# Linear-attention block with a gated MLP: joined feature stores and loads, and another order of the pair loop

## The chip, the cores and the metric

The kernel runs on one core of a Trainium2 chip. The metric is the time of one execution in device microseconds. Before the change it is 2499.09 us (median of 3 runs, 2498.96 to 2500.07).

## The reference

```python
xn = _layernorm(x)                                    # x: 2048 tokens x 1024
q, k, v = split(xn @ wqkv)                            # 32 heads of 32
pq, pk = q @ w_phi, k @ w_phi                         # per head, 32 x 32
phi_q = concat(softmax(pq), softmax(-pq))             # 64 features a head
phi_k = concat(softmax(pk), softmax(-pk))
kv, z = phi_k.T @ v, sum over tokens of phi_k         # per head
o = (phi_q @ kv) / (phi_q @ z + 1e-6)
s = o @ wo
g = silu(((sigmoid(xn @ w_gate)) * (xn @ w_up)) @ w_down)   # 3584 hidden
return x + s * g
```

All in float32. Every large product is made of three matmuls: each operand is split in a high part (rounded to the matmul's float32 form) and the low rest, and hi x hi, hi x lo and lo x hi are added up (`mm3`, L148).

## The kernel before, in words

Large matrix products go through a seven-product scheme (Strassen's in Winograd's form) on blocks of 2 x 2. The seven products are named B11, T2, T3, B21, T1, T4, B22. B11, T2, T3 and T1 open a bank of PSUM; B21 adds on to B11's bank, T4 to T3's, B22 to T1's. In the product with `wo` these four banks are banks 4 to 7, in the order in which the products open them.

The stages, in order: layer norm and the K and V projections; the Q projection; gate and up projections with the gated product in several passes; then the two stages that the change touches.

**The down stage** (from L1820 on) is the product with `w_down`: 112 steps (`dsteps`), each with one block of weights and one or two blocks of hidden values, loaded from DRAM (`down_load`, L941) and split by ScalarE and VectorE (`down_prep`, L959). The first 84 steps have two halves of 12 matmuls each, the last 28 one half. Between halves the kernel calls `tick()` (L178), a clock of the program: `later(n, f)` (L160) puts work n ticks ahead, and all of a tick's work comes, in program order, after what the engines were given before it. So this order, and not the time at which data are there, sets the order of SP's DMA queue and of the other engines.

Beside the steps, `q_late` (L1016) makes the query features of one token tile t of 128 tokens (16 of them) and one half hb of the heads: 32 calls, started every 4.8 ticks (L1874). Six token tiles ("light") have their exponentials from earlier and only load them; ten ("heavy") load q and compute them. Steps at ticks from the start: loads (0 or 6), the exponentials (5 to 11, heavy only), a product with the feature sums (`weigh`, POOL, 11), its reduction (`density`, DVE, 14), the denominators (POOL, 15), their inverses (DVE, 16), the scaling (POOL, 17), `turn` (20), `parted` (21) and `keep` (23). `turn` (L1073) is a VectorE transpose of 32 x 32 blocks of the 128 x 1024 tile into a buffer of the ring `etr`, four slots of 4 KB a partition (20 to 23), two for each call, so that a slot comes back two calls later. `parted` (L1077) splits it in high and low part. `keep` (L1081) stores both, four DMAs each: the DMA c takes 256 columns of all 128 partitions (128 KB) to 32 rows of the DRAM tensor `et_d`, whose row is cut in four pieces of 256 elements (1 KB):

```python
nc.sync.dma_start(et_d[t, hb, a, c * DH:(c + 1) * DH].rearrange("f (a x) -> a f x", a=4),
                  hold[part][:, c * 256:(c + 1) * 256])
```

The weights `wo` lie split in DRAM (`wo_d`, seven sets of four blocks of 512 KB). `wo_prep` (L1105) loads them to the slots in `WO` (L1097): B11's and T2's at steps 40 to 55 of the down stage, T3's and B21's near its end, T1's and T4's into the slots that the last steps free, B22's in the first pair.

**The pair loop** (L1956 to L2069) takes the token tiles two at a time, eight pairs. In pass p, TensorE makes the 28 products of pair p with `wo` (seven names, four blocks each, three matmuls of 128 x 512 each) and the eight numerators of pair p + 1 (`numerators`, L1120: four matmuls of 128 x 256 each, for half hb of the heads, quarter q of them and half b). The features for the numerators of one (hb, q) are loaded by `e_load(q)` (L1110) into slots 44 and 45 (q = 0) or 20 and 21 (q = 1): four DMAs of 256 KB, in pieces of 128 elements (512 B). There is one buffer for each q, so a load waits until the numerators with the last features are done. ScalarE copies one half of a numerator's bank, VectorE adds the other (`numerators_out`, L1130: cp, ad), GpSimd makes the four sums of the operands (`o_sum`, L1139: s11, sA, sB, sC), and `o_part` (L1147) splits an operand. Results are added up by ScalarE and VectorE (`product_out`, L1979), multiplied by g and added to x on GpSimd (`scaled`, L1996), and stored.

The order on all five queues is written out by hand: `PAIR` for a pass, `LAST` for the last pair. A name in it is one of: gB110 (product B11, block 0), nm001 (numerator hb 0, q 0, b 1), cp, ad (its copy and addition), e10 (`e_load` for hb 1, q 0), x...h and x...l (an operand's high and low part), v (a product's result out), m and a (times g, plus x), l (loads of g and x), y (store), w (a block of B22's weights). A name that ends in "-" belongs to the pair before, "+" to the pair after. SP, too, issues in this order: a load that waits holds up what stands behind it. `attend` (L1158) makes the first pair's operands before the loop.

## Time and profile before

| what | value |
|---|---|
| median of 3 runs | 2499.09 us |
| profiled execution: time, span | 2500.76 us, 2499.0 us |
| mean granted TensorE clock | 0.973 |
| busy: PE, DVE, ACT, POOL | 94%, 67%, 49%, 49% of the span |
| DMA: bytes, mean rate | 664.88 MB, 266 GB/s |
| feature stores (`et_d<-x`, L1084) | 256 of 128 KB, first issued at 1646.7 us, last at 2194.6 us |
| feature loads (`<-et_d`, L1116) | 128 of 256 KB, 2203.9 to 2455.2 us |

How to read it: PE is TensorE, DVE VectorE, ACT ScalarE, POOL GpSimd, SP the engine that issues all DMAs here (SPq is its queue). A row of busy times has, for each engine, busy microseconds and the number of instructions, then the granted TensorE clock (1 is full), the mean busy share of the core's 16 DMA engines (overlapping packets can take it a little above 1), and the GB/s that they moved. A row of the timeline has its start, its length, engine and line, operation, output and input, and in brackets the idle time before it and what ended that. "fb", "x", "fa", "fc", "p" and "w" are groups of slots; in the pair loop the buffer for q = 0 is in "fb", that for q = 1 in "x". Successive matmuls overlap, so start to start is the time that one takes.

### The profile page before, as it was taken

What the parts mean: (1) busy time and instruction counts of PE and PEld (TensorE: products, weight loads), DVE (VectorE), ACT (ScalarE), POOL (GpSimd) and SP (SyncE); (2) the same over time, 40 slices, a digit from 0 to 9 for tenths busy, and PEclk for the clock granted to TensorE, in tenths of its full rate; (3) what the DMA queues carried; (4) which work ended last, traced back from release to release, by engine and by line L of the source; (5) the groups of instructions that cost most, each with busy time, mean ns of one, the idle gap of its engine ahead of it and who ended that gap; (6) DMA issues with size and microseconds to landing.
All of it is one profiled execution on the core that took longest, in us unless ns stands there. A gap on an engine that the chain in (4) does not pass through costs nothing.

```text
span 2499.0 us, 31982 instructions
## 1 busy us (share of the span) xinstructions
PE 2354.3 (94%) x10533; PEld 1938.6 (78%) x10533; DVE 1676.8 (67%) x1927; ACT 1217.1 (49%) x1881; POOL 1213.9 (49%) x941
## 2 busy tenths in 40 slices
PE   9999999999999999999999999997978878778888
PEld 8888888888888888888888888886766766666666
DVE  7525777867888657778666566577767677555554
ACT  7345577776446555545555555333433342343331
POOL 1233537841320455656357667475644556314545
PEclk9999999999999999999999999998999989888999
DMA  8789969987887778888787667866655656689875
GB/s 294 266 304 375 351 234 337 349 300 265 290 278 260 278 261 302 293 295 290 252 291 239 228 224 277 332 241 207 233 199 197 209 202 219 217 287 316 239 236 175
DMA packets 382775, 664.88 MB, mean 266 GB/s; under 512 B 38032, under 2 KB 136592, under 8 KB 378000
## 3 DMA queue, kind: packets, MB, share of 16 engines
q1 hardware_dynamic: 382608, 662.84, 76.7%
q8 instruction: 82, 1.34, 0.2%
q14 instruction: 85, 0.70, 0.1%
HBM read 395.12 MB, written 267.58 MB: 265 GB/s over the span
## 4 chain that ended last, share of the span: by engine, by line
PE 66%; DMA 16%; DVE 6%; SPq 4%; POOL 3%; issue 3%; ACT 1%; DVEq 0%; ACTq 0%; POOLq 0%
PE bank L150 21%; PE bank L152 21%; PE bank L151 21%; DMA et_d<-x 4%; DMA fa<-h_d 2%; SPq L1084 2%; DVE w L142 2%; DMA x<-et_d 1%; DMA x<-e_d 1%; PE bank L385 1%; PE bank L748 1%; SPq L1116 1%; POOL fc L1142 1%; DMA fc<-qkv_d 1%; DMA fb<-et_d 1%
## 5 line engine op out<-in xcount | busy, mean ns | idle before, releaser
L151 PE MATMUL bank<-x,w 128*128 128x512 f32 x2248 | 891.5, 397 | 48.0 <-DVE x L142 47.9
L150 PE MATMUL bank<-x,w 128*128 128x512 f32 x2248 | 887.4, 396 | 41.1 <-ACT x L141 9.2
L152 PE MATMUL bank<-x,w 128*128 128x512 f32 x2248 | 884.6, 395 | 4.5 <-DVE w L142 4.5
L142 DVE TENSOR_TENSOR w<-fa,w 128x512 fp32r<-128x512 f32 (+2 forms) x344 | 392.9, 1146 | 276.8 <-ACT w L141 271.5
L151 PEld LDWEIGHTS bank<-x,w 128*128 128x128 f32 x2248 | 430.3, 191 | 146.7 <-DVE x L142 58.3
L150 PEld LDWEIGHTS bank<-x,w 128*128 128x128 f32 x2248 | 430.0, 191 | 135.9 <-ACT x L141 10.0
L152 PEld LDWEIGHTS bank<-x,w 128*128 128x128 f32 x2248 | 430.1, 191 | 95.1 <-DVE w L142 5.6
L141 ACT CAST w<-fa 128x512 fp32r<-128x512 f32 (+2 forms) x344 | 272.6, 795 | 266.0 <-PE bank L151 108.6
L150 PE MATMUL bank<-w,x 128*128 128x512 f32 x704 | 277.3, 394 | 0.0
L152 PE MATMUL bank<-w,x 128*128 128x512 f32 x704 | 276.2, 392 | 0.0
L151 PE MATMUL bank<-w,x 128*128 128x512 f32 x704 | 275.8, 392 | 0.0
L152 PEld LDWEIGHTS bank<-w,x 128*128 128x128 f32 x704 | 133.2, 189 | 28.6 <-DVE x L1299 1.1
L151 PEld LDWEIGHTS bank<-w,x 128*128 128x128 f32 x704 | 133.3, 189 | 26.5
L150 PEld LDWEIGHTS bank<-w,x 128*128 128x128 f32 x704 | 133.4, 189 | 26.3
L142 DVE TENSOR_TENSOR x<-fb,x 128x512 fp32r<-128x512 f32 (+1 forms) x121 | 120.9, 1002 | 25.7 <-ACT x L141 22.8
L1078 ACT CAST x<-x 128x1024 fp32r<-128x1024 f32 x32 | 33.5, 1048 | 171.7 <-DVE x L1075 148.4
L141 ACT CAST x<-fb 128x512 fp32r<-128x512 f32 (+1 forms) x121 | 86.4, 716 | 63.0 <-DMA fb<-wd_d 34.7
L142 DVE TENSOR_TENSOR w<-fb,w 128x512 fp32r<-128x512 f32 (+2 forms) x82 | 84.3, 1028 | 40.7 <-ACT w L141 40.4
L1137 DVE TENSOR_TENSOR fc<-fc,bank 64x512 f32<-64x512 f32 x64 | 43.8, 685 | 86.0 <-ACT fc L1135 85.8
L1135 ACT COPY fc<-bank 64x512 f32<-64x512 f32 x64 | 37.2, 582 | 108.0 <-PE bank L1128 107.7
L142 DVE TENSOR_TENSOR p<-fc,p 128x512 fp32r<-128x512 f32 (+1 forms) x68 | 55.6, 828 | 45.8 <-ACT p L141 43.1
L1444 ACT COPY fc<-bank 128x512 f32<-128x512 f32 x116 | 66.6, 583 | 38.6 <-PE bank L152 15.2
(410 smaller groups left out, 3814.0 us busy)
## 6 DMA issues: line engine op xcount, KB each, us to landing
m_d<-fc SPq DMA_DIRECT2D x168, 256.0 KB
fa<-h_d SPq DMA_DIRECT2D x82, 512.0 KB
fa<-wf_d SPq DMA_DIRECT2D x32, 1024.0 KB
x<-m_d SPq DMA_DIRECT2D x128, 256.0 KB
et_d<-x SPq DMA_DIRECT2D x256, 128.0 KB
fa<-w_gu SPq DMA_DIRECT2D x102, 256.0 KB
h_d<-fc SPq DMA_DIRECT2D x102, 256.0 KB
fc<-qkv_d SPq DMA_DIRECT2D x86, 256.0 KB
```

The costliest lines, as they stand in the source:

```text
L141: nc.scalar.copy(o[0], src)
L142: i = nc.vector.tensor_sub(o[1], src, o[0].bitcast(F32))
L150: nc.tensor.matmul(o, a[0], b[0], start=first, stop=False, **kw)
L151: nc.tensor.matmul(o, a[0], b[1], start=False, stop=False, **kw)
L152: last_mm[:] = [nc.tensor.matmul(o, a[1], b[0], start=False, stop=last, **kw).ins]
L385: nc.tensor.matmul(ps[:, gs], r[:, gs], bd[:, 4 * f + g], start=g == 0, stop=g == 3, skip_group_check=True)
L748: nc.tensor.matmul(kvb[g // 2][:, g % 2 * 256:g % 2 * 256 + 256], v[:, g].rearrange("p a f -> p (a f)"), ph[:, g].rearrange("p a f -> p (a ...
L1078: nc.scalar.copy(hold["hi"].bitcast(F32R), hold["lo"])
L1084: nc.sync.dma_start(et_d[t, hb, a, c * DH:(c + 1) * DH].rearrange("f (a x) -> a f x", a=4), hold[part][:, c * 256:(c + 1) * 256])
L1135: nc.scalar.copy(o, z)
L1137: nc.vector.tensor_add(o, o, y)
L1444: nc.scalar.copy(o, banks[b])
```

## The change

- `et_d` gets another shape: `[8 pairs, 2 parts, 128, 2 tiles of the pair, 2048]`. A row of it now has the pieces of both head halves and both tiles.
- Both head halves of a token tile write into one buffer, a run of two slots for the high and two for the low part. The ring of these buffers is slots 20 to 23 and 8 to 11. `turn` writes at a stride, four pieces of 256 columns.
- `keep` runs only for hb = 1, and for both halves: eight DMAs of 256 KB for each t, two at each of four ticks (23 to 26), in pieces of 512 elements (2 KB). Before it was eight of 128 KB for each t and hb, at one tick. The row is still cut in four pieces (`"f (a y) -> a f y"`, a = 4).
- The calls of `q_late` keep their times, but both halves of a token tile follow each other.
- `e_load` issues two DMAs of 512 KB in place of four of 256 KB, pieces of 512 B as before, now 2 KB apart.
- Since slots 8 to 11 hold features, B11's weights come to them at steps 100 to 107; T1's, not T2's, go to slots 12 to 15 early, at steps 40 to 47, and T2's into slots that the last steps free.
- In `PAIR` the products go B11, T1, T2, T3, B21, T4, B22. The numerators of the first head half stand in the first third of a pass, those of the second after T3. x...T4 moves to the next pass. `attend` splits T1's operand after the first head half. `LAST` is as before.
- Small buffers: `st` has three in place of two; `sa` is smaller, its scaled inverses written over the densities.

```diff
-    et_d = dram.tile([TT, 2, 2, P, 2 * HB], F32, name="et_d")
+    et_d = dram.tile([TT // 2, 2, P, 2, 4 * HB], F32, name="et_d")
...
-    eqr, etr = Ring((50, 51, 24, 25)), Ring((20, 21, 22, 23))
+    eqr, etr, ets = Ring((50, 51, 24, 25)), Ring((20, 8)), {}
...
+        def tile_of(part):
+            return run(ets[t] + 2 * part, 2).rearrange("p a b n -> p (a b n)")
+
+        def half(part):
+            return tile_of(part).rearrange("p (c h x) -> p h c x", c=4, h=2)[:, hb]
+
         def turn():
-            hold["hi"], hold["lo"] = [whole(etr.next()) for _ in range(2)]
-            nc.vector.transpose(hold["lo"], hold["e"])
+            if hb == 0:
+                ets[t] = etr.next()
+            nc.vector.transpose(half(1), hold["e"].rearrange("p (c x) -> p c x", c=4))
...
-        def keep():
-            for a, part in enumerate(("hi", "lo")):
-                for c in range(4):
-                    nc.sync.dma_start(et_d[t, hb, a, c * DH:(c + 1) * DH].rearrange("f (a x) -> a f x", a=4),
-                                      hold[part][:, c * 256:(c + 1) * 256])
+        def keep(part, cs):
+            for c in cs:
+                nc.sync.dma_start(et_d[t // 2, part, c * DH:(c + 1) * DH, t % 2].rearrange("f (a y) -> a f y", a=4),
+                                  tile_of(part)[:, c * HB:(c + 1) * HB])
...
+        if hb:
+            for n in range(4):
+                later(at + 23 + n, keep, n // 2, (2 * (n % 2), 2 * (n % 2) + 1))
...
-    WO = {B11: list(range(8, 12)), T2: list(range(12, 16)), T3: list(range(4, 8)), B21: [],
-          T1: [], T4: [], B22: list(range(4))}
+    WO = {B11: list(range(8, 12)), T1: list(range(12, 16)), T3: list(range(4, 8)), B21: [],
+          T2: [], T4: [], B22: list(range(4))}
...
-                for u in range(2):
-                    o = slots[e_slots[q] + a][:, u].bitcast(F32)
-                    nc.sync.dma_start(o.rearrange("p (a x) -> p a x", a=4),
-                                      et_d[2 * tp_ + u, hb, a].rearrange("p (a q x) -> p q a x", a=4, q=2)[:, q])
+                nc.sync.dma_start(whole(e_slots[q] + a).bitcast(F32).rearrange("p (c x) -> p c x", c=8),
+                                  et_d[tp_, a].rearrange("p u (a h q x) -> p h q (u a) x", a=4, h=2, q=2)[:, hb, q])
...
-        if 40 <= n < 56 and n % 2 == 0:
-            wo_prep(*divmod((n - 40) // 2, 4))
+        if 40 <= n < 48 and n % 2 == 0:
+            wo_prep(T1, (n - 40) // 2)
+        if ND - 12 <= n < ND - 4 and n % 2 == 0:
+            wo_prep(B11, (n - (ND - 12)) // 2)
...
     PAIR = """
-        gB110 mT1- vB22- aT1- lB22- gB111 nm001 cp001 mT4- gB112 nm000 e10 ad001 cp000 aT4- lB21- yT1- gB113 vB11 gT20 nm011
-        ad000 cp011 mB22- yT4- gT21 nm010 e11 ad011 cp010 aB22- lT1- gT22 ad010 yB22- gT23 xB11h vT2 w0 w1 nm101 xB11l cp101
-        gB210 w2 w3 nm100 e00+ s11 ad101 cp100 gB211 gB212 ad100 nm111 cp111 gB213 xT1h nm110 e01+ ad111 cp110 xT1l vB21
-        gT30 ad110 aB21 lT4 gT31 sA xB22h xB22l yB21 gT32 xB21h xB21l gT33 vT3 sB gT10 xT3h xT3l gT11 xT2h gT12 xT2l sC gT13
-        vT1 gT40 xT4h gT41 xT4l gT42 gT43 vT4 gB220 gB221 gB222 gB223""".split()
+        gB110 mT1- vB22- aT1- lB22- nm001 xT4h- xT4l- cp001 gB111 nm000 e10 mT4- ad001 cp000 gB112 gB113 aT4- lB21- yT1- ad000
+        vB11 gT10 nm011 cp011 gT11 nm010 e11 mB22- yT4- ad011 cp010 gT12 gT13 ad010 aB22- lT1- yB22- gT20 xB11h gT21 xB11l
+        gT22 s11 w0 w1 gT23 vT2 xT1h gT30 xT1l gT31 w2 w3 gT32 nm101 cp101 gT33 nm100 e00+ ad101 cp100 vT3 gB210 ad100 vT1
+        gB211 gB212 nm111 cp111 gB213 nm110 e01+ ad111 cp110 vB21 gT40 ad110 aB21 lT4 yB21 gT41 sA xB22h xB22l gT42 xB21h
+        xB21l gT43 vT4 sB gB220 xT3h xT3l gB221 gB222 sC xT2h xT2l gB223""".split()
```

More of the change, by code (lines that the diff above doesn't have):

```diff
@@ L1144, in operands_of @@
     def operands_of(tp_):
-        of[tp_] = {i: ofr.next() for i in (B11, T2, B21, T3, T1, T4, B22)}
+        of[tp_] = {i: ofr.next() for i in (B11, T1, T2, T3, B21, T4, B22)}
     def o_part(tp_, i, part):
@@ L1822, in hedgehog_glu_kernel @@
     block("x3", 12, 4, F32R)
-    for b in range(2):
+    for b in range(3):
         block(f"x{b}", 4 * b, 4, F32)
@@ L1911, in hedgehog_glu_kernel @@
             assert not plan and len(retired) == 2
-            for b in (5, 6):
+            for b in (2, 5, 6):
                 block(f"x{b}", 4 * b, 4, F32R)
@@ L1920, in hedgehog_glu_kernel @@
         if len(dready) == ND:
-            for i, free in ((T1, hfree), (T4, wfree)):
+            for i, free in ((T2, hfree), (T4, wfree)):
                 while free and len(WO[i]) < 4:
```

38 lines of the change are left out of this document (21 added, 17 removed).

## The prediction

> **What bounds the kernel now.** I read the totals first, then busy time by stretches of 50 us.
>
> ```profile
> span 2499.0 us, 31982 instructions
> ```
>
> ```profile
> core 0: us, PE busy (x) PEld busy (x) DVE busy (x) ACT busy (x) POOL busy (x), PEclk, DMA share, GB/s
> ...
> 1650.00:1700.00 50.00, 50.00 (x222) 41.41 (x221) 38.63 (x40) 19.91 (x27) 30.43 (x30) 1.00 0.62 215
> 1700.00:1750.00 50.00, 35.80 (x132) 28.00 (x131) 34.54 (x38) 15.38 (x19) 27.29 (x26) 0.83 0.59 205
> ```
>
> Up to 1700 us PE is full: 222 matmuls in 50 us, 0.225 us each, and nothing done to other engines can gain there. From 1700 us on it loses time. The change touches just that part: the down stage, beside which the features are made and stored, and the pair loop, which loads them. Next come the same view with one stretch for the whole down stage, then its DMA queues.
>
> ```profile
> 1700.00:2200.00 500.00, 413.92 (x1655) 328.89 (x1653) 341.12 (x372) 188.15 (x251) 257.09 (x240) 0.91 0.61 209
> ```
>
> ```profile
> DMA packets 62170, 104.63 MB, mean 209 GB/s; under 512 B 5714, under 2 KB 35339, under 8 KB 62141
> ```
>
> ```profile
> et_d<-x SPq DMA_DIRECT2D x118, 128.0 KB
> ```
>
> ```profile
> et_d<-x SPq DMA_DIRECT2D x114, 128.0 KB
> ```
>
> At 0.225 us the 1655 matmuls need 373 us and got 500. The last two rows are the issues of 1700 to 1950 and of 1950 to 2200: 232 feature stores. A DMA share of 0.61 looks like room; single microseconds show that it isn't.
>
> ```profile
> 1753.00:1754.00 1.00, 1.00 (x5) 0.77 (x5) 1.00 (x3) 1.00 (x2) 1.00 (x1) 0.89 1.06 410
> 1754.00:1755.00 1.00, 1.00 (x6) 0.82 (x5) 1.00 (x1) 0.98 (x2) 0.91 (x3) 1.00 0.94 340
> 1755.00:1756.00 1.00, 1.00 (x6) 0.81 (x5) 1.00 (x3) 0.99 (x3) 0.06 (x1) 1.00 1.02 367
> ...
> 1758.00:1759.00 1.00, 1.00 (x6) 0.84 (x5) 1.00 (x2) 1.00 (x3) 1.00 (x1) 1.00 0.27 99
> ...
> 1764.00:1765.00 1.00, 1.00 (x6) 0.81 (x5) 0.52 (x1) 1.00 (x3) 1.00 (x2) 1.00 0.27 96
> ```
>
> ```profile
> 1755.22 8.54 SPq L1084 DMA_DIRECT2D et_d<-x  x7
> ```
>
> While SP issues a train of feature stores (the seven take 1.22 us each), the share stands at 0.27 of 16 engines: 4.3, so four engines work and twelve are idle, at 96 GB/s. A 128 KB store then takes 131,072 B / 96 GB/s = 1.37 us. Between trains the loads fill all 16 at up to 410 GB/s. I went through all 540 single microseconds from 1650 to 2190. The lowest is the first below, the last one the second:
>
> ```profile
> 1651.00:1652.00 1.00, 1.00 (x6) 0.84 (x5) 1.00 (x3) 0.94 (x3) 1.00 (x2) 1.00 0.23 50
> ...
> 2189.00:2190.00 1.00, 1.00 (x6) 0.81 (x5) 0.87 (x2) 1.00 (x3) 0.00 (x0) 1.00 0.47 171
> ```
>
> None is below 0.23: four engines' worth of work is always under way. Their load can be counted for 1700 to 2200. Stores: 232 x 131,072 B = 30.4 MB, a quarter to each of the four, at 96/4 = 24.0 GB/s: 317 us. The other 74.2 MB, a sixteenth (4.64 MB) to each: the three full rows move 372 GB/s on the mean, 23.3 an engine, the best 410, 25.6; that makes 181 to 199 us. Together 498 to 516 of 500 us. So in the down stage those four engines are the bound; what PE, DVE and SP show as waits follows from them.
>
> In the pair loop I read SP's issues and PE's timeline over one pair. Here L1116 with fb is e_load(0), with x e_load(1), four DMAs each; L1128 are numerators.
>
> ```profile
> 2385.01 2.54 SPq L1116 DMA_DIRECT2D fb<-et_d  x4
> 2387.65 0.63 SPq L1946 DMA_DIRECT2D fc<-g_d  x1
> ...
> 2389.80 3.58 SPq L1116 DMA_DIRECT2D x<-et_d  x4
> ...
> 2415.88 2.55 SPq L1116 DMA_DIRECT2D fb<-et_d  x4
> ```
>
> ```profile
> 2383.29 0.64 PE L1128 MATMUL bank<-fb,p 128*128 128x256 f32 x4
> 2383.76 0.40 PE L150 MATMUL bank<-x,x 128*128 128x512 f32 x1
> ...
> 2384.46 0.64 PE L1128 MATMUL bank<-fb,p 128*128 128x256 f32 x4
> 2384.94 0.40 PE L150 MATMUL bank<-x,x 128*128 128x512 f32 x1
> ...
> 2387.49 0.64 PE L1128 MATMUL bank<-x,p 128*128 128x256 f32 x4
> ...
> 2392.36 0.64 PE L1128 MATMUL bank<-fb,p 128*128 128x256 f32 x3 [2.71 <-DMA fb<-et_d]
> ...
> 2396.78 0.35 PE L1128 MATMUL bank<-x,p 128*128 128x256 f32 x1 [1.23 <-DMA x<-et_d]
> 2398.31 1.01 PE L1128 MATMUL bank<-x,p 128*128 128x256 f32 x3 [1.18 <-DMA x<-et_d]
> ```
>
> ```profile
> 2300.00:2455.00 155.00, 128.57 (x583) 102.92 (x583) 81.03 (x105) 47.45 (x80) 77.44 (x55) 0.95 0.79 237
> ```
>
> From e_load to the same e_load of the next pair is 30.9 us. PE's own work is 84 product matmuls (28 products of 3 x 0.225 = 0.68 us) and 8 numerators of four matmuls (2383.29 to 2383.76: 0.47 us): 19.0 + 3.8 = 22.8 us. The other 8.1 us are the three waits shown (5.1 us), smaller ones, and matmuls at a reduced clock (0.95 on the mean). The wait is latency: the buffer of q=0 is released at 2384.94, its next numerators begin to run through at 2392.36, 7.4 us later, with only five products and two numerators, about 4.3 us, between. Bandwidth: 237 GB/s x 30.9 us = 7.3 MB a pair.
>
> **The change, part by part.**
>
> *Joined stores.* 256 stores of 128 KB become 128 of 256 KB; the bytes are the same, and the runs double from 1 to 2 KB. The view of a store is as before: 32 rows of the tensor cut in four pieces, the four outermost. So I leave it on four engines. What may improve is the rate of one engine: below, no gain (24.0 GB/s); above, the loads' best row, 410/16 = 25.6 GB/s. All 33.6 MB, 8.4 MB an engine: 350 us at 24.0, 328 at 25.6. I take 24.8, in the middle: 339, so -11 us (0 to -22). The Trainium skill has a rule that bears on it ("DMA: Bandwidth & Descriptors", section "Why a DMA increments its semaphore by 16 and not by 1"): a DMA is split over the largest number of engines, up to 16, that divides the slowest dimension of both access patterns. By that rule four pieces mean four engines, in the new stores as in the old, and the trace's 0.27 agrees; it speaks against any gain from joining as such.
>
> *Spread.* A train was 8 stores at one tick for each (t, hb), 8 x 1.37 = 10.9 us; now 16 old stores' worth, 21.8 us, goes out over four ticks once for each t. The four engines have the same work, so the mean does not move. SP's waits get shorter and more; the DVE transposes that waited for a slot get slots 8 to 11 besides 20 to 23, twice the room. That wait is this row:
>
> ```profile
>   DMA et_d<-x: 44.6, 10
> ```
>
> These 44.6 us aren't a gain of their own: with the four engines full, the next late thing is a load of h_d or w_down behind the same stores. The first store moves from tick 25 to 29 (a tick is 12 matmuls, 2.7 us): 10.9 us in which the four engines carry only loads, which fill about half at full pace (190 of 500 us, x 500/373: 0.51). Lost: +5.3 us. The third `st` buffer and the smaller `sa` cost nothing: they add no instruction, and DVE has 341 of 500 us.
>
> *Weights of wo.* Two sets of four were loaded before 1700 us, where PE is full and hides them:
>
> ```profile
> x<-wo_d SPq DMA_DIRECT2D x8, 512.0 KB
> ```
>
> Now T1's is, and B11 (4 x 512 KB = 2.1 MB) comes at steps 100 to 106, after 2200 us, since slots 8 to 11 hold features until then. There DMA is full, with nothing to hide it:
>
> ```profile
> 2200.00:2290.00 90.00, 72.36 (x308) 58.66 (x309) 51.70 (x70) 37.81 (x65) 27.40 (x19) 0.87 0.99 319
> ```
>
> 2.1 MB / 319 GB/s = +6.6 us (0 if a wait elsewhere covers it). T2's set takes the late place that T1's had; it is needed some 7 us earlier in pair 0 (after 8 products and 4 numerators, not 16 and 8), in the same full stretch, at no further bytes.
>
> *Joined loads.* Four DMAs of 256 KB become two of 512 KB; pieces stay 512 B, and all 128 rows are outermost, as before. SP saves at most half of 2.54 us; I count nothing, since bytes and landing stay.
>
> *New order of a pair.* Counting 0.68 and 0.47 us along the new list: q=0 released at 2.3, used at 12.1, released at 13.7, used in the next pair at 23.5; q=1 at 6.0, 15.7, 17.4, 27.1. Each load has 9.8 us in place of 4.3, against 7.4. But SP's order puts lB22- ahead of the first load and lB21-, yT1- ahead of the second, and these wait for POOL: after nm110 come aB21, sA, sB, sC, mT1-, aT1-, at these prices (two sums, a gate product, an addition):
>
> ```profile
> 2405.41 3.31 POOL L1142 TENSOR_TENSOR fc<-fc 128x512 f32<-128x512 f32 x2 [0.69 <-DVE fa L1156]
> ...
> 2409.94 1.67 POOL L2004 TENSOR_TENSOR fc<-fc 128x512 f32<-128x512 f32 x1 [1.23 <-DVE fc L1994]
> 2411.70 1.29 POOL L2005 TENSOR_TENSOR fc<-fc 128x512 f32<-128x512 f32 x1
> ```
>
> Six of 1.3 to 1.7 us and 2 us for numerator, copy and addition: 10.9 us after nm110 at 17.4, 5.5 us into the next pair. After lB22- (0.8 us) the load starts at 6.3 and lands at 13.7, 1.6 late. mT4-, aT4-, lB21- and yT1- put the second at 9.5: it lands at 16.9, needed at 15.7 + 1.6, in time. So 22.8 + 1.6 = 24.4 us; DMA needs 7.3 MB / 319 GB/s = 23.0 of them, so some queueing, of which I take +0.6: 25.0 a pair. Bounds: 23.0, DMA's floor, to 27 (the q=1 load above took from 2387.96 to 2398.31, 10.3 us, 2.9 above 7.4; if that comes on top of 24.4). Six passes, those after the full stretch: 6 x 5.9 = -35.4 us. Pass 0 lies in the full stretch: 0. The last pair keeps its list; T2's operand is ready about 2.2 us into it, needed at 2.7: 0.
>
> **Sum.** -11 + 5.3 + 6.6 - 35.4 = -34.5 us. The profiled execution took 2500.76 us (span 2499.0), the median of three is 2499.09; the sum is a difference, so 2499.1 - 34.5 = 2464.6, say 2465 us. Ends: -22 + 5.3 + 0 - 6 x 7.9 = -64, 2435; 0 + 5.3 + 6.6 - 6 x 3.9 = -11.5, 2488.
>
> **Rivals.**
>
> 1. The pair loop stays tied to POOL and SP: each buffer's landing, a little late, moves nm110 and with it the next POOL chain. For: the first load is late even as worked out. Against: POOL is busy 77 of 155 us. At 28 us a pair, -17.4 + 0.9 = -16.5: 2483 us.
>
> 2. Longer trains starve PE (slower). Now 21.8 us of stores come in 4 ticks of 9.6; in the other 5.6 (15.1 us at full pace) the four engines have 7.7 us of loads. If PE stands still behind the train until its backlog is gone, they idle up to 7.4 us a token tile; it decides as soon as less than 7.4 us of backlog is left at the train's end. At half, 16 x 3.7 = +59 us: 2465 + 59 = 2524. For: peaks double. Against: none of 540 microseconds idles now, and slots for features double.
>
> 3. The loads become slower: 512 B pieces now lie 2 KB apart in rows of 16 KB. No row shows such a pattern. If that eats the 5.9 us of a pair (its 4.2 MB at 220 GB/s rather than 319), only 0.9 us is left: 2500, the same.
>
> 4. The stores do spread over 16 engines. Then the four's 507 us fall to 190 + 317/4 = 269, PE's 373 binds, and up to 127 us go: 2350. Against: the view keeps its four pieces.
>
> **Chances.** Forecast 0.62, rival 1 0.18, rival 2 0.11, rival 3 0.06, rival 4 0.03. What a measurement of this kernel can tell from no change is about 0.2%, 5 us. Faster: 0.62 + 0.18 + 0.03 = 0.83; same 0.06; slower 0.11. The range is 2435 to 2490: the forecast's ends and rival 1 with the stores at no gain; 0.80 lies inside.
>
> **What would show it.** Right: 128 issues of et_d of 256 KB at 2.6 to 2.7 us each in a train, the share still 0.27 there at 96 to 102 GB/s; the down stage still some 500 us long; e_load to e_load 24 to 26 us with waits of about 1 us on et_d. Wrong: single microseconds under 0.2 in the down stage (rival 2), waits on et_d of 2 us and more (rival 1 or 3, told apart by GB/s in a load), a share near 1 during stores (rival 4).

## The result, and the profile after

After the change the median is 2476.29 us (four runs, 2474.06 to 3875.62), before it 2499.58 us (four runs, 2498.96 to 2505.3). The ratio is 0.9899, with a 95% interval of 0.9879 to 0.9918: faster by about 1%. The run of 3875.62 us, whose mean granted clock was 0.556 where the other three have 0.974 to 0.978, is left out of the ratio. The profiled execution took 2474.06 us.

The page after, in its first and its sixth part (span; feature stores, now at L1091):

```profile
span 2472.3 us, 31667 instructions
...
et_d<-x SPq DMA_DIRECT2D x128, 256.0 KB
```

Busy time by stretches after: the down stage, then a single microsecond in it. The last columns are the granted TensorE clock, the DMA share and GB/s.

```profile
1700.00:2200.00 500.00, 411.51 (x1642) 327.47 (x1641) 336.60 (x371) 186.53 (x250) 252.37 (x241) 0.90 0.61 211
```

```profile
1761.00:1762.00 1.00, 1.00 (x6) 0.84 (x5) 1.00 (x2) 1.00 (x3) 1.00 (x1) 1.00 0.27 104
```

As a whole the stretch is as it was: 1642 matmuls in its 500 us, against 1655 before. Cut at 2150 us it isn't. First before, then after:

```profile
1700.00:2150.00 450.00, 370.30 (x1475) 294.15 (x1473) 311.77 (x334) 165.75 (x215) 242.66 (x229) 0.90 0.61 210
2150.00:2250.00 100.00, 82.90 (x346) 66.80 (x347) 57.62 (x80) 46.48 (x80) 23.07 (x17) 0.90 0.79 261
```

```profile
1700.00:2150.00 450.00, 375.34 (x1510) 299.82 (x1508) 316.07 (x347) 170.24 (x222) 245.58 (x236) 0.91 0.60 210
2150.00:2250.00 100.00, 73.98 (x280) 57.13 (x281) 42.96 (x58) 34.96 (x60) 13.13 (x10) 0.86 0.78 262
```

From 1700 to 2150 us PE does 35 matmuls more than before, and in the 100 us behind that 66 fewer. During a store the share still stands at 0.27, so four engines carry the joined stores too. Over 1650 to 2190 us, 168 such microseconds (share 0.24 to 0.28) move 100.8 GB/s on the mean; 198 of them before moved 96.8. New is that these four engines now stand idle at times. Before, one single microsecond of the 540 had a share under 0.24; after, 15 have, most of them here:

```profile
1725.00:1726.00 1.00, 0.24 (x2) 0.00 (x0) 0.00 (x0) 0.00 (x0) 1.00 (x3) 1.00 1.00 389
...
1729.00:1730.00 1.00, 0.00 (x0) 0.00 (x0) 1.00 (x2) 0.18 (x1) 1.00 (x3) 0.61 0.21 82
...
1731.00:1732.00 1.00, 0.00 (x0) 0.00 (x0) 1.00 (x2) 1.00 (x2) 1.00 (x2) 0.50 0.00 0
...
1735.00:1736.00 1.00, 0.89 (x2) 0.79 (x3) 1.00 (x2) 1.00 (x2) 0.91 (x2) 0.50 0.00 0
...
1740.00:1741.00 1.00, 1.00 (x6) 0.82 (x5) 1.00 (x1) 0.00 (x0) 1.00 (x2) 1.00 0.83 203
```

PE stands still there too. One row each of the timelines of PE, VectorE and POOL after leads from the wait to its start (in brackets: the idle time before, and what ended it), and two of SP's queue show the loads that POOL waited for:

```profile
1735.12 0.80 PE L151 MATMUL bank<-x,w 128*128 128x512 f32 x1 [9.87 <-DVE x L142]
```

```profile
1728.54 1.25 DVE L1082 STREAM_TRANSPOSE x<-fc 128x1024 f32<-128x1024 f32 x1 [9.57 <-POOL fc L1071]
```

```profile
1723.77 1.29 POOL L898 TENSOR_TENSOR fb<-fb 128x512 f32<-128x512 f32 x1 [21.77 <-DMA fb<-w_down]
```

```profile
1707.17 3.05 SPq L1091 DMA_DIRECT2D et_d<-x  x2
...
1712.68 1.15 SPq L908 DMA_DIRECT2D fb<-w_down  x2
```

The loads of `w_down` stand in SP's queue behind stores and are issued at 1712.68. POOL waited 21.77 us for them, with the features' scaling (L1071) behind that sum in its queue; VectorE's transpose waited 9.57 us for the scaling, with a split of the weights (L142) and three more steps between behind it; and PE waited for this split. From 1731 to 1736 nothing is loaded and nothing stored.

The last activation of the down stage (its end, for all that follows) before and after:

```profile
2257.59 0.63 ACT L1837 ACTIVATE p<-x 128x512 f32<-128x512 f32 x1
```

```profile
2262.27 0.63 ACT L1846 ACTIVATE p<-x 128x512 f32<-128x512 f32 x1
```

So the changed kernel is 4.7 us late when the pair loop begins, and gains all it gains behind that. The pair loop after, as busy time, as e10 loads of passes 1 and 6 in SP's queue (L1124), and as PE's waits for the numerators' features in 2300 to 2455 us (total, times, longest):

```profile
2300.00:2455.00 155.00, 144.74 (x688) 119.15 (x687) 103.31 (x124) 54.65 (x92) 95.85 (x67) 0.98 0.93 277
```

```profile
2295.36 1.27 SPq L1124 DMA_DIRECT2D fb<-et_d  x2
...
2427.97 1.24 SPq L1124 DMA_DIRECT2D fb<-et_d  x2
```

```profile
PE bank L1136 <- DMA x<-et_d: 8.3, 8, 1.5
PE bank L1136 <- DMA fb<-et_d: 1.4, 3, 0.7
```

Before, the same e10 loads and PE's waits in the same 155 us were these:

```profile
2292.30 2.55 SPq L1116 DMA_DIRECT2D fb<-et_d  x4
...
2447.16 2.54 SPq L1116 DMA_DIRECT2D fb<-et_d  x4
```

```profile
PE bank L1128 <- DMA fb<-et_d: 17.4, 7, 3.6
PE bank L1128 <- DMA x<-et_d: 8.0, 8, 1.3
```

From e10 to e10 after are 132.61 us in five passes, 26.5 each; before, 154.86 us, 31.0 each. The wait that went is the one for q = 0 (17.4 to 1.4 us); that for q = 1 stayed (8.0 and 8.3). PE runs 688 matmuls in 155 us in place of 583, and DMA moves 277 GB/s in place of 237.

### The profile page after: what moved, and what is told of

The parts are those of the page before. It is cut to its first block, busy times and chain, and to the rows that moved or that the text cites. A ratio compares the mean times of both kernels' runs of the same rounds, so it can differ in the third digit from the quotient of the medians.

```text
span 2472.3 us, 31667 instructions
## 1 busy us (share of the span) xinstructions
PE 2346.6 (95%) x10533; PEld 1936.0 (78%) x10533; DVE 1670.5 (68%) x1927; ACT 1217.0 (49%) x1879; POOL 1213.5 (49%) x941
## 4 chain that ended last, share of the span: by engine, by line
PE 70%; DMA 15%; DVE 5%; POOL 4%; SPq 3%; issue 2%; ACT 0%; DVEq 0%; POOLq 0%; ACTq 0%
PE bank L150 22%; PE bank L151 22%; PE bank L152 22%; DMA et_d<-x 3%; DMA x<-e_d 2%; DMA fa<-h_d 2%; DMA x<-et_d 1%; PE bank L748 1%; DVE w L142 1%; POOL fc L1043 1%; PE bank L385 1%; DMA fb<-et_d 1%; DMA fb<-wd_d 1%; DMA fc<-e_d 1%; SPq L1091 1%
## 5 line engine op out<-in xcount | busy, mean ns | idle before, releaser
L142 DVE TENSOR_TENSOR w<-fa,w 128x512 fp32r<-128x512 f32 (+2 forms) x344 | 397.9, 1161 | 295.5 <-ACT w L141 279.4
L142 DVE TENSOR_TENSOR x<-fb,x 128x512 fp32r<-128x512 f32 (+1 forms) x121 | 119.9, 992 | 58.8 <-ACT x L141 58.5
L150 PEld LDWEIGHTS bank<-w,x 128*128 128x128 f32 x704 | 132.3, 188 | 26.3
L142 DVE TENSOR_TENSOR w<-fb,w 128x512 fp32r<-128x512 f32 (+2 forms) x82 | 79.6, 972 | 48.8 <-ACT w L141 48.8
L142 DVE TENSOR_TENSOR p<-fc,p 128x512 fp32r<-128x512 f32 (+1 forms) x68 | 53.8, 802 | 41.4 <-ACT p L141 39.3
L141 ACT CAST w<-fb 128x512 fp32r<-128x512 f32 (+2 forms) x82 | 50.1, 611 | 61.9 <-PE bank L151 37.3
L1150 POOL TENSOR_TENSOR fc<-fc 128x512 f32<-128x512 f32 x32 | 48.8, 1525 | 51.4 <-DVE fb L1164 24.5
```

Source lines behind the costliest of these rows:

```text
L141: nc.scalar.copy(o[0], src)
L142: i = nc.vector.tensor_sub(o[1], src, o[0].bitcast(F32))
L150: nc.tensor.matmul(o, a[0], b[0], start=first, stop=False, **kw)
L1150: nc.gpsimd.tensor_sub(o, a, b)
```

## The experiments

Theory A, formed from these rows: the four engines still bound the down stage, the joined transfers bring nothing or cost some us, and the new order of the pair brings the whole gain. The rivals: the joined loads shorten the pair; the joined stores' better rate makes the gain; and, for the stage, something other than the four engines bounds it.

One table for all twelve, since they are read against each other. The ratio is to the kernel before, run on the same chip, with its 95% interval. The third column is the last activation of the down stage in the profiled run, the fourth the mean of passes 1 to 5 (e10 to e10). Executions of one kernel lie 2 to 9 us apart, and these two columns come from one execution each, so a few us in the third are not a result by themselves.

| kernel | ratio | stage ends, us | pass, us |
|---|---|---|---|
| before | 1 | 2257.6 | 31.0 |
| changed | 0.9899 (0.9879 to 0.9918) | 2262.3 | 26.5 |
| 1 order alone | 0.9883 (0.9869 to 0.9898) | 2257.3 | 27.2 |
| 2 joined transfers alone | 1.0027 (1.0017 to 1.0037) | 2264.3 | 31.1 |
| 3 order, stores by rows | 0.9349 (0.9333 to 0.9364) | 2122.7 | 26.8 |
| 4 changed, stores by rows | 0.9349 (0.9335 to 0.9363) | 2124.5 | 26.3 |
| 5 order, numerators at old places | 1.0033 (1.0021 to 1.0045) | 2256.3 | 31.9 |
| 6 order, B11's weights late | 0.9876 (0.9861 to 0.9891) | 2255.7 | 27.2 |
| 7 changed, stores at one tick | 0.9942 (0.9929 to 0.9954) | 2272.7 | 26.2 |
| 8 changed, loads in four | 0.9913 (0.9899 to 0.9927) | 2270.3 | 26.8 |
| 9 changed, halves stored apart | 0.9882 (0.9867 to 0.9897) | 2264.6 | 26.7 |
| 10 numerators moved alone | 0.9897 (0.9881 to 0.9914) | 2258.6 | 27.1 |
| 11 as 3, quarters apart in DRAM | 0.9443 (0.9429 to 0.9457) | 2160.2 | 25.4 |
| 12 as 3, loads in whole runs | 0.9308 (0.9294 to 0.9322) | 2123.7 | 25.8 |

### 1. The order alone

On the kernel before, with the new `PAIR` and what belongs to it; stores and loads as before:

```diff
+    WO = {B11: list(range(8, 12)), T1: list(range(12, 16)), ..., T2: [], T4: []}
...
-            wo_prep(*divmod((n - 40) // 2, 4))
+            wo_prep((B11, T1)[(n - 40) // 8], (n - 40) // 2 % 4)
...
-        gB110 mT1- vB22- aT1- lB22- gB111 nm001 cp001 mT4- ...
+        gB110 mT1- vB22- aT1- lB22- nm001 xT4h- xT4l- cp001 ...
```

> The kernel before with the new order of the pair's products alone (with the operands' order, the numerators half a pair apart, and the early weights of T1); B11's weights stay in the middle of the down stage, and stores, their ticks and the loads of the features are those of before. Theory A (the order makes the gain): passes 1 to 5 shorten from 30.9 to some 26.5 us as in the changed kernel, the down stage keeps its 500 us, and what the changed kernel lost up to the first pair's first products (3.1 us) is not lost here: 2499.6 - 29.8 = about 2470 us (2462 to 2478). Theory B (the joined loads shorten the pair): the passes stay at 30.9 us, 2499 us. Theory C (half and half): about 2485 us.

Measured: 2470.71 us, ratio 0.9883. The loads e10 of passes 1 and 6 in its trace:

```profile
2288.92 3.00 SPq L1116 DMA_DIRECT2D fb<-et_d  x4
...
2424.86 2.54 SPq L1116 DMA_DIRECT2D fb<-et_d  x4
```

135.94 us in five passes, 27.2 each, with the old loads of four DMAs. The order alone gives the whole gain; theory B (2499) and theory C (2485) are out.

### 2. The joined transfers alone

The changed kernel with the old `PAIR`, operand order and places of the weights:

```diff
-        gB110 mT1- vB22- aT1- lB22- nm001 xT4h- xT4l- cp001 ...
+        gB110 mT1- vB22- aT1- lB22- gB111 nm001 cp001 mT4- ...
...
-            wo_prep(T1, (n - 40) // 2)
+            wo_prep(T2, (n - 40) // 2)
```

B11's late weights stay, since slots 8 to 11 hold features here too.

> The changed kernel with the order of the pair's products, of its operands and of the weights put back to that of before: joined and spread stores, joined loads and the late weights' place of before stay as the one part that is tried. Theory A (the order makes the gain, the joined transfers none): the down stage ends some 5 us later or at the same time, passes stay near 30.9 us (with the loads' own price at most 1 us less each): 2497 to 2505 us. Theory B (the joined loads shorten the pair): passes at 26.5 us, 2475 us. Theory C (the joined stores shorten the down stage by their whole change of rate, 13.6 us): about 2486 us with passes of 30.9 us.

Measured: 2508.12 us, ratio 1.0027: slower than before by 4 to 9 us, a little past theory A's range. Its first store and its loads e10:

```profile
1658.39 3.62 SPq L1091 DMA_DIRECT2D et_d<-x  x4
```

```profile
2299.02 1.24 SPq L1124 DMA_DIRECT2D fb<-et_d  x2
...
2454.75 1.24 SPq L1124 DMA_DIRECT2D fb<-et_d  x2
```

The first store comes 11.7 us later than before (1646.73 there). 165 store microseconds move 100.6 GB/s, but 15 others have a share under 0.24. The stage ends 6.7 us later, and the passes (31.1 us) are those of before. Theories B and C are both out.

### 3 and 4. The stores by rows

The same bytes in as many DMAs, but each takes 32 partitions with all their four pieces, so the outermost index of the view counts 32 rows and not four pieces. On experiment 1's kernel and on the changed one:

```diff
-                for c in range(4):
-                    nc.sync.dma_start(et_d[t, hb, a, c * DH:(c + 1) * DH].rearrange("f (a x) -> a f x", a=4),
-                                      hold[part][:, c * 256:(c + 1) * 256])
+                for g in range(4):
+                    nc.sync.dma_start(et_d[t, hb, a].rearrange("(c f) y -> f c y", c=4)[:, :, g * 256:(g + 1) * 256],
+                                      hold[part][g * DH:(g + 1) * DH].rearrange("f (c x) -> f c x", c=4))
```

```diff
-                nc.sync.dma_start(et_d[t // 2, part, c * DH:(c + 1) * DH, t % 2].rearrange("f (a y) -> a f y", a=4),
-                                  tile_of(part)[:, c * HB:(c + 1) * HB])
+                nc.sync.dma_start(et_d[t // 2, part, :, t % 2].rearrange("(c f) y -> f c y", c=4)[:, :, c * HB:(c + 1) * HB],
+                                  tile_of(part)[c * DH:(c + 1) * DH].rearrange("f (c y) -> f c y", c=4))
```

> The first experiment's kernel with its stores cut another way: each of the four DMAs of a part takes 32 partitions with all their four pieces, so that the outermost index of the transfer counts 32 rows and not 4 pieces; bytes, number of DMAs, ticks and destinations are the same. Theory A (the four engines that carry the stores bound the down stage): the share of the 16 engines rises above 0.27 in the stage, PE's waits go, and the stage shrinks from 500 us towards PE's own busy time of 373 us in it; with VectorE's 414 us of busy time as the next bound, 50 to 100 us go: 2370 to 2420 us. Rival (the engines stand for something else, and the stage is bound by VectorE, ScalarE and their semaphores): within 10 us of the first experiment, 2460 to 2480 us. The Trainium skill, page DMA: Bandwidth & Descriptors, section Why a DMA increments its semaphore by 16 and not by 1, has the number of engines follow the outermost index, and would give 16 engines here.

> The changed kernel with its joined stores cut by rows in the same way: each DMA takes 32 partitions with all four of their 2 KB pieces. Theory A (four engines bound the down stage): as in the third experiment, 50 to 100 us less than the changed kernel, 2376 to 2426 us, and the share of the DMA engines is spread over 16 of them. Rival (not the engines): 2470 to 2480 us.

Measured: 2336.01 and 2337.7 us, both 0.9349 of before: 135 us under experiment 1 and 139 under the changed kernel, more than the 50 to 100 expected. Three views of experiment 3: the stores in the page (with 3.7 us from issue to landing), the stage by busy time, and single microseconds that lie within or at the end of trains of stores (SP issued four from 1748.14, four from 1750.83 and seven from 1761.83 us on).

```profile
et_d<-x SPq DMA_DIRECT2D x256, 128.0 KB, 3.7
```

```profile
1750.00:2100.00 350.00, 349.75 (x1551) 289.39 (x1550) 317.61 (x344) 175.77 (x242) 233.33 (x206) 1.00 0.88 284
```

```profile
1753.00:1754.00 1.00, 1.00 (x6) 0.81 (x6) 1.00 (x2) 0.01 (x1) 1.00 (x1) 1.00 0.81 307
1754.00:1755.00 1.00, 1.00 (x6) 0.84 (x5) 1.00 (x1) 0.00 (x0) 1.00 (x2) 1.00 1.05 372
...
1762.00:1763.00 1.00, 1.00 (x6) 0.83 (x5) 1.00 (x3) 1.00 (x2) 0.54 (x1) 1.00 0.78 180
```

No plateau of 0.27 is left: in these rows the share is 0.78 to 1.05. PE is busy for all of 350 us, at full clock, 0.2255 us a matmul, and DMA moves 284 GB/s, against 209 in 1700 to 2200 us before. The stage ends at 2122.7 us, 134.6 before experiment 1's. Only the cut of the stores was changed, so that their confinement to four engines bounded the stage is shown. One rival is left to answer: with the new cut SP is also held for less time (1.06 us for the median store in experiment 1, 0.44 in 3). But the joined stores hold SP for some 174 us in all, where experiment 1's hold it for at least 275, and the stage isn't shorter for it; so SP's own time was not the bound. The expectation was too low because of a misread row: 414 us is PE's busy time in the stage before; VectorE's is 341. The Trainium skill's rule that the prediction weighed (page "DMA: Bandwidth & Descriptors", section "Why a DMA increments its semaphore by 16 and not by 1": the slowest dimensions of both access patterns set the number of engines) fits in both directions: four pieces outermost gave 0.27, 32 rows up to 1.05 (loads beside them included). Whether the stores are joined no longer matters by then: 3 and 4 have the same ratio.

### 5 and 10. What of the order it is

Experiment 5 keeps the new order of products and puts the second head half's numerators back; experiment 10 keeps the old order of products and moves just these numerators, with the steps that depend on them:

```diff
-        gT22 s11 w0 w1 gT23 vT2 xT1h gT30 xT1l gT31 w2 w3 gT32 nm101 cp101 gT33 nm100 e00+ ad101 cp100 ...
+        gT12 gT13 nm101 cp101 ad010 ... gT20 nm100 e00+ ad101 cp100 ... gT22 ad100 nm111 cp111 ... gT23 nm110 e01+ ...
```

```diff
-        gT23 xB11h vT2 w0 w1 nm101 xB11l cp101 gB210 w2 w3 nm100 e00+ s11 ad101 cp100 ...
+        gT32 nm101 cp101 gT33 nm100 e00+ ad101 cp100 vT3 gT10 gT11 ad100 gT12 nm111 cp111 gT13 nm110 e01+ ad111 cp110 ...
```

> The first experiment's kernel (new order alone, 2470.7 us) with the numerators of the second head half moved back to where they stood in the order before: behind 8, 9, 11 and 12 products of a pair instead of 15, 16, 19 and 20. The order of the products stays new. Theory A1 (the distance of a buffer's two uses makes the gain: a load has 4 to 5 products in place of 13 again): the waits on the feature loads return, passes 1 to 5 go from 26.5 to about 30.9 us, 6 x 4.4 = 26 us: 2497 us (2490 to 2502). Rival A2 (the order of the products and of their operands makes it, since POOL's sums get more room): 2471 us, passes of 26.5 us.

> The kernel before (2500 us) with the numerators of the second head half moved half a pair on, to behind 15, 16, 19 and 20 products, and the operands' steps that need them moved behind them; the products keep the order of before, so that the operands of T2 and T3 are ready only shortly before their use. Theory A1 (the distance alone makes the gain): 2468 to 2475 us, passes of 26.5 us. Rival A2 (the distance needs the order of the products as well: with T2 second in a pair, its operand, two sums behind the last numerator, comes late): passes between 28 and 32 us, 2480 to 2505 us.

Measured: 2509.59 us (1.0033) and 2475.95 us (0.9897). The loads e10 of passes 1 and 6, first of experiment 5, then of experiment 10, and PE's waits for features in experiment 5, 2300 to 2455 us:

```profile
2297.67 2.54 SPq L1116 DMA_DIRECT2D fb<-et_d  x4
...
2457.39 2.83 SPq L1116 DMA_DIRECT2D fb<-et_d  x4
```

```profile
2293.78 2.54 SPq L1116 DMA_DIRECT2D fb<-et_d  x4
...
2429.04 2.54 SPq L1116 DMA_DIRECT2D fb<-et_d  x4
```

```profile
PE bank L1128 <- DMA fb<-et_d: 24.0, 9, 3.3
PE bank L1128 <- DMA x<-et_d: 4.2, 4, 1.6
```

With the new products but the old distance a pass takes 31.9 us and the wait on q = 0 is back (24.0 us; the kernel before has 17.4 there). With the old products and the new distance it takes 27.1. So the distance between a buffer's two uses, with the operands' steps that go with it, makes the gain. The order of products by itself, without the distance, is slower than before by 5 to 11 us; beside the distance it adds nothing that these intervals resolve (0.9883 and 0.9897 overlap). Rival A2 of experiment 10 is out: its passes are 27.1 us and not 28 to 32.

### 6. B11's weights late

```diff
-            wo_prep((B11, T1)[(n - 40) // 8], (n - 40) // 2 % 4)
+            wo_prep(T1, (n - 40) // 2)
+        if ND - 12 <= n < ND - 4 and n % 2 == 0:
+            wo_prep(B11, (n - (ND - 12)) // 2)
```

> The first experiment's kernel (2470.7 us) with B11's weights loaded at steps 100 to 107, as in the changed kernel, and not at steps 40 to 47; stores and loads of the features are those of before. The prediction's term for it is +6.6 us (2.1 MB in a stretch where the DMA engines are full): 2477 us. Rival (the 2.1 MB leave the middle of the down stage, where the four engines are full, and a sixteenth of them each, 0.131 MB at 24 GB/s, 5.5 us, is saved there): 2470 to 2472 us.

Measured: 2470.24 us, 0.9876 beside 0.9883 for experiment 1. The late place costs nothing that can be measured; +6.6 is out.

### 7. All joined stores at one tick

```diff
-                later(at + 23 + n, keep, n // 2, (2 * (n % 2), 2 * (n % 2) + 1))
+                later(at + 23, keep, n // 2, (2 * (n % 2), 2 * (n % 2) + 1))
```

> The changed kernel (2476.3 us) with all eight joined stores of a token tile at the first of their four ticks, so that a train carries 2.1 MB, 21 to 22 us of the four engines, in one go. Theory A (the four engines are fed in either way, and only SP's queue is blocked for longer): PE waits more behind each train for loads that stand in SP's queue, and the four engines idle more; up to 16 x 3.7 = 59 us: 2480 to 2535 us; my value 2490. Rival (the stores start up to 3 ticks earlier and the spread was worth nothing): 2468 to 2476 us.

Measured: 2486.38 us, 0.9942: 10 us above the changed kernel, and the intervals (0.9929 to 0.9954, 0.9879 to 0.9918) lie apart. A train of eight now holds SP for 14 us:

```profile
1660.88 14.00 SPq L1091 DMA_DIRECT2D et_d<-x  x8
```

The stage ends 10.4 us later than in the changed kernel, which is the whole difference. It is lost before 2150 us: PE does 1467 matmuls from 1700 us on to there, in place of 1510, and DMA moves 203 GB/s in place of 210. Given joined stores, spreading them is worth 10 us. By which wait they are lost is not shown: 22 single microseconds of the 540 have a share under 0.24, in place of 15, but what they lack to 0.27 is 10.6 us of the four engines' time, hardly more than the changed kernel's 9.4.

### 8. The loads in four again

```diff
-                nc.sync.dma_start(whole(e_slots[q] + a).bitcast(F32).rearrange("p (c x) -> p c x", c=8),
-                                  et_d[tp_, a].rearrange("p u (a h q x) -> p h q (u a) x", a=4, h=2, q=2)[:, hb, q])
+                for u in range(2):
+                    nc.sync.dma_start(slots[e_slots[q] + a][:, u].bitcast(F32).rearrange("p (c x) -> p c x", c=4),
+                                      et_d[tp_, a, :, u].rearrange("p (a h q x) -> p h q a x", a=4, h=2, q=2)[:, hb, q])
```

> The changed kernel (2476.3 us) with each feature load as four DMAs of 256 KB again instead of two of 512 KB, the same pieces of 512 B from the same places. Theory A (the number of DMAs of a load is worth nothing, its bytes and pieces set it): 2474 to 2479 us. Rival (joining the loads gave a part of the gain, SP's 2.5 us for four issues against 1.2 to 1.5 for two, twice a pair and half): six passes of 2 to 4 us more: 2488 to 2500 us.

Measured: 2479.67 us, 0.9913, with an interval that overlaps the changed kernel's. The rival's 12 to 24 us are out; whether fewer DMAs gain some us stays open (3.4 us by the medians, passes of 26.8 against 26.5 us).

### 9. Each half stored by itself

```diff
-                nc.sync.dma_start(et_d[t // 2, part, c * DH:(c + 1) * DH, t % 2].rearrange("f (a y) -> a f y", a=4),
-                                  tile_of(part)[:, c * HB:(c + 1) * HB])
+                    nc.sync.dma_start(et_d[t // 2, part, c * DH:(c + 1) * DH, t % 2].rearrange("f (a h x) -> h a f x", a=4, h=2)[hb],
+                                      tile_of(part)[:, c * HB + hb * 256:c * HB + (hb + 1) * 256])
...
-                                  (21, parted)):
+                                  (21, parted), (23, keep)):
```

> The changed kernel (2476.3 us) with its layout, loads and order, but each head half stored by itself again as soon as it is ready: eight DMAs of 128 KB in pieces of 1 KB at one tick, as in the kernel before. Theory A (joining costs, because the first half waits for the second, the four engines start 13 us later and the stores' better rate doesn't pay for it): the first store is back at about 1647 us and the time at that of the new order alone, 2467 to 2473 us. Rival A' (the gain of rate of 13.6 us is real and is lost too): 2476 + 13.6 - 13 = 2475 to 2480 us, no difference.

Measured: 2472.47 us, 0.9882. The first store is back at its old time, only three microseconds have a share under 0.24, and 206 store microseconds move 96.6 GB/s:

```profile
1646.20 1.26 SPq L1092 DMA_DIRECT2D et_d<-x  x2
```

The time is theory A's, but its interval overlaps the changed kernel's, and in its profiled run the stage ends at 2264.6 us, no earlier than the changed kernel's. So the rate and the late start belong to the joining, as the counts show, but the time of the stage's end does not.

The table shows with what it does go. The five kernels with the layout of the change (changed, 2, 7, 8, 9) end the stage at 2262.3 to 2272.7 us and do 280 to 319 matmuls from 2150 to 2250 us. The five with the old stores and their layout (before, 1, 5, 6, 10) end it at 2255.7 to 2258.6 us and do 341 to 356. Experiment 9 has the loss with the halves stored apart, experiment 8 with the loads in four, and experiment 6 has B11's weights late without the loss. So the loss needs neither joined stores nor joined loads, and B11's late weights don't make it; whether the new order of the token tiles' halves, their slots or the place in DRAM does was not tried.

### 11 and 12. What holds the pair loop

Experiment 11 lays the two quarters of a row apart in DRAM, so that loads read 2 KB runs, at the price of 512 stores of 64 KB in pieces of 512 B. Experiment 12 changes only where the loads read: whole runs, which hold other features than the numerators need, so it prices the pieces and computes something else.

```diff
-                                      et_d[2 * tp_ + u, hb, a].rearrange("p (a q x) -> p q a x", a=4, q=2)[:, q])
+                    nc.sync.dma_start(o, et_d[2 * tp_ + u, hb, a, q])
...
+                    for q in range(2):
+                        nc.sync.dma_start(et_d[t, hb, a, q].rearrange("(c f) y -> f c y", c=4)[:, :, g * 128:(g + 1) * 128],
+                                          hold[part][g * DH:(g + 1) * DH].rearrange("f (c q x) -> f q c x", c=4, q=2)[:, q])
```

```diff
+                    nc.sync.dma_start(o, et_d[2 * tp_ + u, hb, a, :, q * HB:(q + 1) * HB])
```

> The third experiment's kernel (new order, stores cut by rows over all engines: 2336.0 us) with the two quarters of a row apart in DRAM: a feature load reads 2 KB runs, a store is two DMAs of 64 KB in pieces of 512 B. Theory (the pair loop is now at the DMA engines, share 0.93 to 0.97 with 512 B pieces, so longer runs shorten the passes from 26.7 towards PE's 22.8 us, while PE has cover for the shorter pieces in the down stage): six to seven passes of 1.5 to 3 us less: 2316 to 2327 us. Rival (512 DMAs of 64 KB and their shorter pieces fill the down stage, whose share is 0.90 already): 2336 to 2360 us.

> The third experiment's kernel (2336.0 us) whose feature loads read the same number of bytes in whole runs of 2 KB (from the left or right half of each row instead of four pieces of it, so the numerators get wrong features); stores as in the third experiment. It prices the 512 B pieces alone. Theory (the pieces hold the passes at 26.7 us): passes fall to 23.5 to 25 us, 2316 to 2327 us. Rival (the POOL chain, the loads' release and the wait behind it hold them): 2332 to 2338 us.

Measured: 2362.65 and 2328.39 us, against 2336.01 for experiment 3. Loads e10 of passes 1 and 6 of experiments 3, 11 and 12:

```profile
2153.25 3.02 SPq L1116 DMA_DIRECT2D fb<-et_d  x4
...
2287.03 2.74 SPq L1116 DMA_DIRECT2D fb<-et_d  x4
```

```profile
2189.74 2.17 SPq L1117 DMA_DIRECT2D fb<-et_d  x4
...
2316.68 1.81 SPq L1117 DMA_DIRECT2D fb<-et_d  x4
```

```profile
2152.29 1.91 SPq L1116 DMA_DIRECT2D fb<-et_d  x4
...
2281.36 1.96 SPq L1116 DMA_DIRECT2D fb<-et_d  x4
```

PE in the five passes of experiment 12:

```profile
2152.29:2281.36 129.07, 120.96 (x601) 100.86 (x600) 89.58 (x108) 49.25 (x83) 81.59 (x56) 1.00 0.85 294
```

Passes of 26.8, 25.4 and 25.8 us: the pieces of 512 B cost 1.0 to 1.4 us a pass, where I expected passes of 23.5 to 25. In experiment 11 the stores take back far more: the stage ends 37.5 us later than in experiment 3. A row of its SP queue and one of its busy time by stretches:

```profile
1799.22 10.67 SPq L1085 DMA_DIRECT2D et_d<-x  x15
```

```profile
1800.00:1850.00 50.00, 44.13 (x191) 35.14 (x190) 35.51 (x38) 20.91 (x29) 25.16 (x26) 1.00 0.83 236
```

Fifteen stores hold SP for 10.67 us, and PE is no longer full. Whether SP's queue is the cause, or the smaller pieces on the engines, was not tried. So the stores of experiments 3 and 4 are the version to keep; both are faster than the changed kernel too (0.9349 against 0.9899).

## Why the prediction was right, and where it was not

It said 2465 us, range 2435 to 2490; it came to 2476.29. Its direction and the main term hold; the sum was -34.5 and the medians differ by -23.3. The profiled spans differ by -26.7 us: +3.1 up to the first e10 of pass 1, -22.3 in passes 1 to 5, -7.5 behind them.

- **Four engines bound the down stage.** Shown (3, 4). The prediction priced rival 4 at up to 127 us for a store that spreads over 16 engines; such a store gave 135. Why the profile could tell: PE's 413.92 us for 1655 matmuls were 0.250 us each, not 0.225. Of the 127 us that the stage lost, 86 were idle and 41 were slower matmuls (the mean granted clock was 0.91, and 0.225/0.91 is 0.247), and a full PE gets both back.
- **The joined stores' rate, -11 us.** 33.55 MB at 96.8 GB/s are 346.6 us, at 100.8 GB/s 332.9: -13.7. The term holds, as work of the four engines.
- **The late first store, +5.3 us.** The store came 12.8 us later (1659.53 against 1646.73), where 4 ticks of 2.7 us are 10.8. Up to 2150 us the two terms come out: -13.7 + 5.3 = -8.4, and PE's 35 matmuls more are some 8 us at 0.225 us (in experiments 2 and 8 only 13 and 15 more).
- **The end of the stage, no term.** From 2150 to 2250 us PE does 66 matmuls fewer, some 15 us at 0.225 us, and the stage ends 4.7 us later in spite of the lead. The sum had no such loss. It comes with the changed layout as a whole (9); its cause stays open. The joined part is a loss of 4 to 9 us by itself (2), where the prediction's terms for it, -11 + 5.3 + 6.6, made +0.9.
- **The spread.** What failed is "The four engines have the same work, so the mean does not move": at times the four engines do stand idle (15 microseconds in place of one, ten of them under 0.2, the prediction's own sign of rival 2). Rival 2's mechanism is there, at a small size: what those 15 lack to 0.27 adds up to 9.4 us of the four engines' time. Another 10 us go when the spread is taken away (7), though not as idle time counted like this. The issues of 256 KB took 0.62 us on the median and 2.35 each in the longest train (five in 11.75 us), not 2.6 to 2.7.
- **B11's weights, +6.6 us: wrong, 0** (6). "There DMA is full, with nothing to hide it" counted the late stretch and not the one that the weights left, which is just as full on the four engines that count. A transfer that leaves that stretch frees its sixteenth on each of the four (0.131 MB at 24 GB/s, 5.5 us); that this is what cancels the 6.6 fits the result, but was not tried by itself.
- **Joined loads, 0.** Not shown to differ from 0 (8); rival 3 is out, since the passes at 2 KB pitch (26.5 us) are no longer than at 1 KB (27.2).
- **The new order, -35.4 us.** Experiment 1 gives 0.9883 of 2501 us, -29 us. The mechanism was right: the distance from a buffer's release to its use (5, 10). The size was off, since a pass came to 26.5 us and not 25.0. Two steps failed. One is "it lands at 16.9, needed at 15.7 + 1.6, in time": of the waits left, 8.3 us in 155 us (5.8 passes, so 1.4 a pass) are for q = 1, the second load, and 0.24 a pass for the first, which I had 1.6 us late. That the two add up to the 1.6 us is luck. The other is 22.8 us for PE's own work: it is busy 24.8 us a pass (144.74 in 155 us). I took every matmul at full clock, although the prediction had read a mean of 0.95 in the old passes. Here are PE's waits for q = 1 in one pass after, and two matmuls behind them:

```profile
2361.75 0.35 PE L1136 MATMUL bank<-x,p 128*128 128x256 f32 x1 [1.48 <-DMA x<-et_d]
2363.26 0.62 PE L1136 MATMUL bank<-x,p 128*128 128x256 f32 x3 [1.16 <-DMA x<-et_d]
...
2365.52 0.63 PE L150 MATMUL bank<-x,x 128*128 128x512 f32 x1
2365.95 0.63 PE L151 MATMUL bank<-x,x 128*128 128x512 f32 x1
```

They start 0.43 us apart; the granted clock is 0.50 in the microsecond 2365. But the clock isn't all of it: at a mean clock of 1.00 (12) PE is still busy 24.2 us a pass (120.96 in five). What the other 1.4 us are was not looked into. And I let the DMA engines run at 319 GB/s, while the pieces of 512 B cost a pass 1 us (12). The POOL steps that time the loads add up to 11.2 us by the rows shown, not 10.9, from which nothing follows.

- **Pass 0, 0 us: wrong.** It went from 33.9 us (e10 from 2258.39 to 2292.30) to 26.8 (2268.57 to 2295.36): -7.1. Its start (the first e10) had moved 10.2 us later, so up to pass 1 the net is +3.1 us, where the terms made +0.9. That these two are close is luck: the sum had neither the 10.2 nor the 7.1.

## What to carry to other kernels

A mean DMA share of 0.61 can hide four engines that are full beside twelve that are not half busy, as the prediction's count has it here: look at single microseconds during each kind of transfer, and if a plateau of k/16 shows, cut the transfer so that its outermost index counts many rows, before making transfers larger or spreading them. In a loop whose order is written out by hand, put the two uses of a single buffer half a loop apart; that alone was worth some 26 us here (10), and the order of the products beside it nothing that could be measured. Fewer and larger stores are no gain by themselves: here they started 12.8 us later, and eight in one train held SP's queue, with the loads behind them, for 14 us (7).

## What the runs showed of the hardware

- A store that reads only 32 of the 128 partitions isn't held to a few engines: within and right behind such trains the rows of experiment 3 show shares of 0.78 to 1.05 and up to 372 GB/s, loads beside them included, where the other cut holds 0.27 and 104. How much of that is the stores' own was not separated.
- Taken over four engines, one engine moves 24.2 GB/s (96.8/4) in pieces of 1 KB and 25.2 GB/s (100.8/4) in pieces of 2 KB.
- The granted clock follows PE's pauses. In the rows after, PE stops at 1725.2, the clock leaves 1.00 within the microsecond 1729 (mean 0.61) and stands at 0.50 from 1730 on, PE starts again at 1735.12, and the clock is at 1.00 from 1740. At 0.50 matmuls start 0.43 us apart (2365.52 and 2365.95), at 1.00 0.225 us. The Trainium skill, page "TensorE: Matmul & The Clock Gate", section "Part 1: The HAM clock gate", has the rate halve after an idle window of about 3.4 us. The 4 us here agree, and the half rate too. But a pause in one piece isn't needed: after waits of 1.48 and 1.16 us with a single matmul between (PE is busy 0.28, 0.25 and 0.11 of the microseconds 2360 to 2362) the clock falls to 0.55 in 2364 and 0.50 in 2365. It makes such waits cost more than their own time: PE's busy time over the whole kernel fell from 2351.5 us (1) to 2305.1 us (3) for the same 10533 matmuls, at a mean granted clock of 0.974 and 0.995.
